# Three quarters of w_out among x's pages and the fourth behind its second reading, the last T copied out of four tiles by two engines, and loads released by the table's landing

## The chip, the cores and the metric

The kernel runs on one core of a Trainium2 chip. The metric is device time in microseconds (us); "before" is the tuned kernel, "after" the same kernel with the change. TensorE is PE (its weight loads PEld), VectorE is DVE, ScalarE is ACT, GpSimd is POOL, and SP is the engine that issues nearly all DMAs.

## The reference

All in float32, with the three parts chained:

```
X = fft(fft(x, axis=1), axis=2).real        # x: [8, 3072, 256] -> 24576 rows of 256
logits = X @ phi                            # 8 experts, 4 slots each: 32 columns
d = softmax(logits, over the rows)          # dispatch, per slot
slot_in = d.T @ X                           # [32, 256]
slot_out[e] = relu(slot_in[e] @ w1[e]) @ w2[e]     # w1[e] 256x1024, w2[e] 1024x256
y = softmax(logits, over the slots) @ slot_out     # [24576, 256]
out = (s * relu(y @ w_in)**2 + b) @ w_out   # w_in 256x2048, w_out 2048x256
```

## The kernel before

The transform is never written out. The program has a prologue of about 206 us and a main loop of about 1177 us (lines L1140, L1170 and L1173, which multiply the 24576 rows with w_in and w_out and are not touched by the change). The prologue runs through these stages:

- **x stage** (0 to about 82 us): 24 pages of x (`xb`, 1 MB each, three per batch of the eight) are multiplied by projected phi and transform tables (`vt`, L419), copied to `vts` (L428), transposed (`vq`, L437), copied to `v` (L441), and multiplied by a transform table into `tps` (L472). ACT or DVE copies `tps` to the table T (`tt`, L484 or L486), eight copies a batch. The last batch has a way of its own (`emit_t(B-1)`, L445 to L470): a tile `tpa` (L450), which ACT copies in eight pieces (L454), and a tile `tpb` (L461), which DVE copies in two (L467). Two matmuls of `keep_busy` on a `warm` tile (L194) stand behind them.
- **lp stage** (about 85 to 98): `lp` (L592) multiplies `tt` with the table `ltab` to the logits, in 16 tiles; DVE takes a maximum of each (L605) and ACT copies it (L606).
- **h stage** (99 to 117) and **r stage** (117 to 179): `hp` (L668) and `htp` (L721), then for each n `dps` (L729), DVE's copy `dh` (L734), and the sum `racc` (L744) over x, which is read a second time in pages `xrt`.
- **e stage** (180 to 206): the sum goes to `rsb` (DVE L886 and ACT L887), through `rtp`, `rt`, `sip` and `si` to the experts: `e_up` (`ehp`, L944, ACT's `hs` L949), `e_turn` (`etp`, L965) and `e_down` (`eop`, L976).

All pages (`xb`, `xrt`, `w1t`, `w2t`, `wi`, `wo`) come from one ring of page buffers, and SP issues their DMAs in program order. Each DMA waits until the eighth before it has landed, and until the last reader of its page is through. `ORDER` is a string of the loads in the x stage: `x` a page of x, `w` a quarter of w_out, `s` a store of `ltab`, `r` a page of `xrt`, `l` a piece of `lt`, `h` a part of `htab`; in `todo` stand those of the r stage.

w_out comes in four quarters of 1 MB (`wo_load(k)`, `raw`). Each has side steps, which `side_step` places between other work: DVE takes the two halves of the words apart (L154, L158, L162, L166, L174; `double_steps`), finds their maxima (L227) and scales (L209, L210), ACT casts a high half (L217, twice), DVE forms a low half (L221, twice), and POOL adds the rows into `bias` (L281, four times). The maxima over all four are then joined (`late_steps`: L258, `mx` L262 and L267, L263, L268) beside `e_up`. `htab_fetch` (L363 to L367) loads the second table `htab_t`; POOL's 1x1 memset (L365) in it is what the load waits for.

Of the kernel before, what the change touches and what calls it, by code (L numbers as in the profile page):

```python
# [32 lines left out]
def tile_fft2__then__softmoe__then__act_relu2(  # L33
# [149 lines left out]
    wo, wi, wok, wik, whl = [], [], [], [], []  # L183
# [13 lines left out]
    def wo_load(k):  # L197
        if k % 2 == 0:
            t, kk = page([P, 8, D], F32, "wo")
            wo.append(t)  # L200
            wok.append(kk)
            whl.append(page([P, 8, 2, D], F16, "whl")[0])
        w = wo[k // 2][:, 4 * (k % 2):4 * (k % 2) + 4, :]
# [29 lines left out]
        steps += [(0.0, lambda j=j: low(j), 0.65) for j in range(2)]  # L233
# [67 lines left out]
    ORDER = "xxxwxxxxxxwxxxxxxwxxxxwxsrllhh"  # L301
    tpool = tc.alloc_tile_pool(name="tpool", bufs=1)
    doubles += [((3, 1, 3, 1)[k], lambda k=k: wo_load(k)) for k in range(4)]
# [88 lines left out]
    with tc.tile_pool(name="xtp", bufs=1, side="right") as xtp, tc.tile_pool(name="vp", bufs=1, side="right") as vp, \  # L392
# [52 lines left out]
        def emit_t(b):  # L445
            bg, bq = divmod(b, NG)
            if b == B - 1:
                t = psv.tile([P, 4, P], F32, tag="vq", name="tpa", bufs=2)
                for k in range(4):
                    nc.tensor.matmul(t[:, k, :], lhsT=vs[bg][:, bq, 4 * k:4 * k + 4, :].rearrange("p j n -> p (j n)"),  # L450
                                     rhs=f_sb, start=True, stop=True)
                for j in range(4):
                    for c in range(2):
                        nc.scalar.copy(tt[64 * bg + NR * c:64 * bg + NR * c + NR, :, bq, 8 * j:8 * j + 4],  # L454
                                       t[NR * j:NR * j + NR, :, 64 * c:64 * c + 64].rearrange("p e k -> p k e"))
                t = psv.tile([P, 2, 4, 64], F32, tag="vt", name="tpb", bufs=2)
                for k in range(4, 8):
                    for j in range(4):
                        for c in range(2):
                            q = 64 * (j // 2) + NR * c  # L460
                            nc.tensor.matmul(t[q:q + NR, j % 2, k - 4, :], lhsT=vs[bg][:, bq, 4 * k + j, :],  # L461
                                             rhs=f_sb[:, 64 * c:64 * c + 64], start=True, stop=True,
                                             tile_position=(0, q), skip_group_check=True)
                for eh in range(2):
                    src = t[64 * eh:64 * eh + 64].rearrange("p j k m -> p m j k")
                    dst = tt[64 * bg:64 * bg + 64, :, bq, 16 * eh:16 * eh + 16].rearrange("p m (j k) -> p m j k", j=2)
                    nc.vector.tensor_copy(dst[:, :, :, 4:8], src)  # L467
# [29 lines left out]
        keep_warm(psv.tile([P, 4 * P], F32, tag="vt", name="warm", bufs=2)[:, :P], 16)  # L497
# [31 lines left out]
        nc.gpsimd.tensor_copy(ltabs[1][0][0:64], ltabs[0][0][64:P])  # L529
# [3 lines left out]
        load_xr()  # L533
        nc.gpsimd.tensor_copy(ltabs[1][0][64:P], ltabs[0][0][0:64])
# [6 lines left out]
        keep_busy(psv.tile([P, 4 * P], F32, tag="vt", name="warm", bufs=2), 4 * P)  # L541
        keep_busy(psv.tile([P, 4 * P], F32, tag="vt", name="warm", bufs=2), P)
# [39 lines left out]
    with tc.tile_pool(name="ps_l", bufs=6, space=PSUM) as psl:  # L582
# [33 lines left out]
        side_step(0.0, True)  # L616
# [18 lines left out]
    with tc.tile_pool(name="ps_h", bufs=3, space=PSUM) as psh:  # L635
# [25 lines left out]
        for i in range(-3, NCH + 1):  # L661
# [170 lines left out]
    todo += [(1, load_xr)] * 2  # L832
# [18 lines left out]
    for n in range(NST + 2):  # L851
# [12 lines left out]
        if n in (1, 2):  # L864
            side_step(0.0, True)
# [463 lines left out]
```

## Time and profile before

| | |
|---|---|
| time of three runs (us) | 1384.62 median, 1384.21 to 1385.57 |
| profiled execution: its own time, its span (us) | 1384.65, 1382.8 |
| busy in the span: PE, DVE, ACT, POOL | 99%, 85%, 73%, 17% |
| mean granted TensorE clock | 0.999 |
| HBM read, written (MB) | 78.50, 26.21 |

The span runs from the first to the last instruction; the profiled execution's own time is 1.85 us longer than it. Busy shares are means over prologue and main loop, and a busy PE need not be PE at its peak. Nearly all the reading from HBM falls in the prologue, so the sections below speak of stretches of the prologue alone.

### The profile page before, as it was taken

To read this page: it belongs to the slowest core of one execution; us is meant where nothing else is said; L and a number is where in the kernel's file an instruction comes from. 1 tells how busy PE (TensorE), PEld (TensorE's weight loads), DVE (VectorE), ACT (ScalarE), POOL (GpSimd) and SP (SyncE) were. 2 spreads that over 40 slices of the span, in tenths; PEclk is the share of its full clock that TensorE was granted. 3 is DMA by queue.
4 is the path that set the end of the run, shared out by engine and by line. 5 is a ranking of instruction groups with operands and counts; after the bars stand their busy time and mean duration, and the time that the engine had idled before them with its cause. 6 is when DMAs were issued, how large, how long until landed. Compare 5 with 4: busy or idle time off the path is not lost.

```text
span 1382.8 us, 22960 instructions
## 1 busy us (share of the span) xinstructions
PE 1366.6 (99%) x8974; PEld 829.6 (60%) x8974; DVE 1171.4 (85%) x1491; ACT 1007.4 (73%) x1413; POOL 231.4 (17%) x287
## 2 busy tenths in 40 slices
PE   8999999999999999999999999999999999999998
PEld 6666555656656666566666666665666666656665
DVE  2587828998989898989898989989888989888886
ACT  2785128877878777877777877777777777777774
POOL 1246001121212121212121211111111111111110
PEclk9999999999999999999999999999999999999999
DMA  9989980101010101010101010110101010101000
GB/s 384 412 312 405 416 349 24 28 24 34 24 36 21 37 24 37 23 35 22 35 24 35 22 37 24 29 29 24 36 21 37 21 36 23 38 24 34 23 22 29
DMA packets 72460, 112.27 MB, mean 81 GB/s; under 512 B 34096, under 2 KB 59696, under 8 KB 64928
## 3 DMA queue, kind: packets, MB, share of 16 engines
q1 hardware_dynamic: 72320, 110.78, 23.0%
q8 instruction: 70, 1.15, 0.3%
q14 instruction: 38, 0.31, 0.1%
q0 software_dynamic: 32, 0.03, 0.0%
HBM read 78.50 MB, written 26.21 MB: 76 GB/s over the span
## 4 chain that ended last, share of the span: by engine, by line
PE 89%; DMA 8%; DVE 2%; SPq 1%; ACT 0%; issue 0%; DVEq 0%; ACTq 0%
PE op L1170 47%; PE op L1173 24%; PE fhp L1140 12%; DMA xb<-in_x_turned_dram 3%; PE racc L744 3%; DMA w2t<-in_moe_w_dram 2%; DMA raw<-in_moe_w_out_dram 1%; PE hp L668 1%; DMA lt<-in_ltab_dram 1%; PE dps L729 1%; DVE cm L605 1%; SPq L1103 0%; DMA ltab<-lt 0%; DVE r L1146 0%; DVE rhl L1131 0%
## 5 line engine op out<-in xcount | busy, mean ns | idle before, releaser
L1170 PE MATMUL op<-whl,rhl 128*128 128x512 f16 x3072 | 1025.5, 379 | 0.8 <-ACT rhl L1130 0.6
L1173 PE MATMUL op<-whl,rhl 128*128 128x256 f16 x3072 | 836.2, 273 | 0.0
L1145 ACT ACTIVATE r<-fhp,wsc 128x768 f32<-128x768 f32 (+1 forms) x513 | 461.4, 900 | 230.8 <-PE fhp L1140 229.8
L1146 DVE SCALAR_TENSOR_TENSOR r<-fhp,r 128x768 f32<-128x768 f32 (+1 forms) x513 | 488.5, 952 | 114.1 <-ACT r L1145 104.0
L1131 DVE TENSOR_TENSOR rhl<-r,rhl 128x768 f16<-128x768 f32 x511 | 506.1, 990 | 0.9 <-ACT rhl L1130 0.9
L1170 PEld LDWEIGHTS <-rhl 128*128 128x128 f16 x3072 | 299.7, 98 | 336.6 <-ACT rhl L1130 0.9
L1130 ACT CAST rhl<-r 128x768 f16<-128x768 f32 x511 | 420.2, 822 | 1.8 <-DVE r L1146 1.8
L1173 PEld LDWEIGHTS <-rhl 128*128 128x128 f16 x3072 | 300.6, 98 | 62.3 <-issue 0.3
L1185 POOL TENSOR_TENSOR ot<-ot,bias 128x256 f32<-128x256 f32 x189 | 137.9, 730 | 974.4 <-DVE ot L1183 974.4
L1140 PE MATMUL fhp<-ct,g 128*128 128x384 f16 x1024 | 250.8, 326 | 1.1 <-DMA g<-gs 0.8
L1140 PEld LDWEIGHTS <-g 128*128 128x128 f16 x1024 | 99.8, 98 | 69.1 <-issue 1.5
L1182 ACT ACTIVATE o<-op,small 128x256 f32<-128x256 f32 x189 | 89.7, 475 | 16.5 <-PE op L1173 16.5
L1183 DVE SCALAR_TENSOR_TENSOR ot<-op,small,o 128x256 f32<-128x256 f32 x192 | 91.4, 476 | 0.3
L419 PE MATMUL vt<-xb,phd 128*64 128x384 f32 (+3 forms) x288 | 47.6, 467 | 4.3 <-DMA xb<-in_x_turned_dram 3.9
L744 PE MATMUL racc<-xrt,dh 128*64 128x256 f32 x384 | 44.5, 383 | 0.4 <-DVE dh L734 0.4
L419 PEld LDWEIGHTS vt<-xb,phd 128*64 128x64 f32 x288 | 25.3, 137 | 24.5 <-issue 7.5
L744 PEld LDWEIGHTS racc<-xrt,dh 128*64 128x64 f32 x384 | 26.3, 137 | 20.9 <-issue 4.1
L486 ACT COPY tt<-tps 32x512 f32<-32x512 f32 x48 | 27.7, 576 | 5.1 <-PE tps L472 4.6
L441 DVE COPY v<-vq 128x512 f32<-128x512 f32 (+1 forms) x15 | 8.3, 593 | 23.8 <-PE vq L437 23.8
L428 ACT COPY vts<-vt 128x512 f32<-128x512 f32 (+1 forms) x15 | 8.0, 535 | 27.6 <-PE vt L419 27.5
L791 POOL TENSOR_TENSOR lg<-lg,rm 112x512 f32<-112x512 f32 x16 | 22.4, 1405 | 5.8 <-DVE rm L789 5.8
L773 POOL TENSOR_TENSOR lg<-et,lg 112x512 f16<-112x512 f32 x16 | 18.5, 1159 | 0.0
(234 smaller groups left out, 480.8 us busy)
## 6 DMA issues: line engine op xcount, KB each, us to landing
xb<-in_x_turned_dram SPq DMA_DIRECT2D x24, 1024.0 KB, 20.2
xrt<-in_x_pages_dram SPq DMA_DIRECT2D x24, 1024.0 KB, 11.6
out_dram<-ot SPq DMA_DIRECT2D x128, 128.0 KB, 1.7
w1t<-in_moe_w_dram SPq DMA_DIRECT2D x8, 1024.0 KB, 13.8
out_dram<-ot SPq DMA_DIRECT2D x128, 64.0 KB, 2.0
raw<-in_moe_w_out_dram SPq DMA_DIRECT2D x4, 1024.0 KB, 20.3
raw<-in_moe_w_in_dram SPq DMA_DIRECT2D x4, 1024.0 KB, 9.3
w2t<-in_moe_w_dram SPq DMA_DIRECT2D x4, 1024.0 KB, 16.8
```

Of the source, the lines that this page charges most:

```text
L419: nc.tensor.matmul(vt[64 * h:64 * h + 64, o:o + k, :], lhsT=phd[:, c, sg, :], rhs=turned(pg, c, i, k, rev), start=(c == 0 and m < 2), stop ...
L744: nc.tensor.matmul(raccs[acc][64 * h:64 * h + 64, :], lhsT=dh[:, m, g].rearrange("p j e -> p (j e)"), rhs=xr[k][0][:, g, t, :], start=(sum ...
L1130: nc.scalar.copy(a, r2)
L1131: nc.vector.tensor_tensor(out=l, in0=r2, in1=a, op=ALU.subtract)
L1140: nc.tensor.matmul(hp[k * split][:, k, :].rearrange("p (s b m) -> p s b m", s=2, b=B), lhsT=g16[:, f * P:(f + 1) * P], rhs=c, start=True, ...
L1145: nc.scalar.activation(out=r[:, k], in_=hp[i][:, k], func=AF.Relu, scale=wsc[:, 2, p:p + 1])
L1146: nc.vector.scalar_tensor_tensor(out=r2[:, k], in0=hp[i][:, k], scalar=0.0, in1=r[:, k], op0=ALU.max, op1=ALU.mult)
L1170: nc.tensor.matmul(op.rearrange("p h d -> p (h d)"), lhsT=a, rhs=w.rearrange("p h d -> p (h d)"), start=(f == 0), stop=False)
L1173: nc.tensor.matmul(op[:, 0, :], lhsT=l, rhs=w[:, 0, :], start=False, stop=(f == NFC - 1))
L1182: nc.scalar.activation(out=o1, in_=op[:, 1, :], func=AF.Copy, scale=qv)
L1183: nc.vector.scalar_tensor_tensor(out=ot, in0=op[:, 0, :], scalar=qv, in1=o1, op0=ALU.mult, op1=ALU.add)
L1185: nc.gpsimd.tensor_tensor(out=ot, in0=ot, in1=bias, op=ALU.add)
```

## The change

Five edits, all in the prologue.

1. `ORDER` has three `w` in place of four, the first behind the eighth `x` of the string instead of the third. Quarter 4 (k = 3) is loaded in `todo`, behind the last `xrt` and ahead of the first `w1t`. Quarters 3 and 4 have `wo` pages of their own; the low halves of quarter 3 go to steps 8 and 10 of the h stage.
2. `emit_t(B-1)` uses two tiles `tpa` and two tiles `tpb`; ACT and DVE each copy one of either kind.
3. In `htab_fetch` the 1x1 memset is a 1x1 copy from `ltabs[0]`, and POOL's first copy of `ltab` comes behind the loads instead of ahead of them.
4. The warm-up at the start is 28 matmuls with 64 moving columns instead of 16 with 128; the two `keep_busy` ahead of `lp` are gone.
5. The side step behind `mt` and those at n = 1 and 2 of the r stage are gone, and the `late_steps` stand further back in the e stage.

```diff
-        w = wo[k // 2][:, 4 * (k % 2):4 * (k % 2) + 4, :]
+        w = wo[0][:, 4 * k:4 * k + 4, :] if k < 2 else wo[k - 1]
...
-        steps += [(0.0, lambda j=j: low(j), 0.65) for j in range(2)]
+        if k == 2:
+            late_low.extend(lambda j=j: low(j) for j in range(2))
+        else:
+            steps += [(0.0, lambda j=j: low(j), 0.65) for j in range(2)]
...
-    ORDER = "xxxwxxxxxxwxxxxxxwxxxxwxsrllhh"
+    ORDER = "xxxxxxxxwxxxxxxwxxxwxxxsrllhh"
...
-        nc.gpsimd.memset(t[0:1, 0, 0, 0:1], 0.0)
+        nc.gpsimd.tensor_copy(t[0:1, 0, 0, 0:1], ltabs[0][0][0:1, 0, 0:1])
...
-                t = psv.tile([P, 4, P], F32, tag="vq", name="tpa", bufs=2)
+                for m in range(2):
+                    t = psv.tile([P, 4, P], F32, tag="vq", name="tpa", bufs=2)
...
+                    for j in range(4):
+                        for c in range(2):
+                            r = 64 * bg + NR * c
+                            (nc.vector.tensor_copy if m else nc.scalar.copy)(
+                                tt[r:r + NR, :, bq, 8 * j + 2 * m:8 * j + 2 * m + 2],
+                                t[NR * j:NR * j + NR, 0:2, 64 * c:64 * c + 64].rearrange("p e k -> p k e"))
+                ts = [psv.tile([P, 2, 4, 64], F32, tag="vt", name="tpb", bufs=2) for _ in range(2)]
...
-                    nc.vector.tensor_copy(dst[:, :, :, 4:8], src)
+                    (nc.vector.tensor_copy if eh else nc.scalar.copy)(dst[:, :, :, 4:8], src)
...
-        keep_warm(psv.tile([P, 4 * P], F32, tag="vt", name="warm", bufs=2)[:, :P], 16)
+        keep_warm(psv.tile([P, 4 * P], F32, tag="vt", name="warm", bufs=2)[:, :P // 2], 28)
...
-        nc.gpsimd.tensor_copy(ltabs[1][0][0:64], ltabs[0][0][64:P])
         for i in range(2):
             htab_fetch(i)
         load_xr()
         load_xr()
+        nc.gpsimd.tensor_copy(ltabs[1][0][0:64], ltabs[0][0][64:P])
...
-        keep_busy(psv.tile([P, 4 * P], F32, tag="vt", name="warm", bufs=2), 4 * P)
-        keep_busy(psv.tile([P, 4 * P], F32, tag="vt", name="warm", bufs=2), P)
...
+            if i in (8, 10):
+                late_low.pop(0)()
...
-    todo += [(1, load_xr)] * 2
+    todo += [(1, load_xr)] * 2 + [(2, lambda: wo_load(3))]
...
-        if n in (1, 2):
-            side_step(0.0, True)
...
-    late_steps.pop(0)()
     for eg in range(2):
         for fh in range(2):
             e_up(eg, fh)
-            late_steps.pop(0)()
             e_side(2.0)
...
+            if eg + fh:
+                late_steps.pop(0)()
```

Three engines' orders show what this moves. **DVE** at the end of the r stage, before (`dh` is the last copy of the r stage, `rsb` the first of the e stage; line numbers differ by up to ten between the kernels):

```order
L245 TENSOR_REDUCE small<-wi 128x1
L258 TENSOR_REDUCE small<-small 128x1
L734 COPY dh<-dps 128x2x4x32
L879 TENSOR_SCALAR small<-zacc 128x1
L880 RECIPROCAL small<-small 128x1
L263 TENSOR_REDUCE small<-mx 1x1
L886 TENSOR_SCALAR rsb<-racc_1156,small 128x256
```

And in the changed kernel:

```order
L740 COPY dh<-dps 128x2x4x32
L154 TENSOR_SCALAR wo<-raw 128x1024
L158 SCALAR_TENSOR_TENSOR wo<-raw,wo 128x1024
L162 SCALAR_TENSOR_TENSOR wo<-raw,wo 128x1024
L883 TENSOR_SCALAR small<-zacc 128x1
L884 RECIPROCAL small<-small 128x1
L166 TENSOR_SCALAR raw<-raw 128x1024
L174 SCALAR_TENSOR_TENSOR wo<-raw,wo 128x1024
L228 TENSOR_REDUCE wsc<-wo 128x2
L890 TENSOR_SCALAR rsb<-racc_1158,small 128x256
```

Six steps of quarter 4 now stand between the last `dh` and `rsb`. Behind `si` DVE's changed order goes on with the rest of that quarter and the joined maximum:

```order
L917 COPY si<-sip 128x64
L210 TENSOR_SCALAR wsc<-wsc 128x2
L211 RECIPROCAL wsc<-wsc 128x2
L222 SCALAR_TENSOR_TENSOR whl<-wo,wsc,whl 128x2x256 x2
L262 TENSOR_REDUCE small<-wsc 128x1
L262 TENSOR_REDUCE small<-small 128x1
L267 TENSOR_REDUCE small<-mx 1x1 x2
```

Before, L258 stood directly behind `si`. **POOL** around the table, before:

```order
L281 TENSOR_TENSOR bias<-bias,wo 128x256 x4
L529 COPY ltab<-ltab 64x2048
L365 MEMSET htab_t 1x1 x2
L534 COPY ltab<-ltab 64x2048
L281 TENSOR_TENSOR bias<-bias,wo 128x256 x4
```

And in the changed kernel, there and then in the e stage, where the last four bias additions now stand behind `sel`:

```order
L285 TENSOR_TENSOR bias<-bias,wo 128x256 x4
L369 COPY htab_t<-ltab 1x1 x2
L540 COPY ltab<-ltab 64x2048
L541 COPY ltab<-ltab 64x2048
L375 COPY htab_t<-htab_t 48x16x52
```

```order
L797 TENSOR_TENSOR lg<-lg,rm 112x512
L932 DMA sel_sb<-in_sel_dram 128x2x32
L934 COPY sel_1775<-sel_sb 128x256
L285 TENSOR_TENSOR bias<-bias,wo 128x256 x4
L1112 COPY g_2000<-gs 32x320 x4
```

The 1x1 copies stand ahead of both copies of `ltab`, and the additions have moved past the h and r stages. **SP** at the second weights `w2t`, with what each DMA waits for (DMAHW0 to DMAHW7 are the landings of the eighth DMA before), before:

```order
L826 DMA w2t<-in_moe_w_dram 128x2048 [waits DMAHW7_49,PE_49]
L826 DMA w2t<-in_moe_w_dram 128x1024 [waits DMAHW0_49,PE_49]
L826 DMA w2t<-in_moe_w_dram 128x1024 [waits DMAHW1_49,PE_49]
L826 DMA w2t<-in_moe_w_dram 128x1024 [waits DMAHW2_49,PE_49]
L826 DMA w2t<-in_moe_w_dram 128x1024 [waits DMAHW3_49,PE_49]
L826 DMA w2t<-in_moe_w_dram 128x1024 [waits DMAHW4_49]
```

And in the changed kernel:

```order
L832 DMA w2t<-in_moe_w_dram 128x2048 [waits DMAHW7_49,PE_49]
L832 DMA w2t<-in_moe_w_dram 128x1024 [waits DMAHW0_49,DVE_49]
L832 DMA w2t<-in_moe_w_dram 128x1024 [waits DMAHW1_49,DVE_49,Pool_49]
L832 DMA w2t<-in_moe_w_dram 128x1024 [waits DMAHW2_49,PE_49]
L832 DMA w2t<-in_moe_w_dram 128x1024 [waits DMAHW3_49]
L832 DMA w2t<-in_moe_w_dram 128x1024 [waits DMAHW4_49]
```

The second of the half-size `w2t` loads takes the page of quarter 4 in `wo`: it waits for that quarter's low halves on DVE and its bias additions on POOL.

## Rows read from the trace of the kernel before

**Rows 1.** Busy time by stretch: us, then each engine's busy (count), clock, DMA share, GB/s.
```profile
6.00:78.00 72.00, 67.69 (x459) 44.72 (x459) 36.71 (x55) 40.94 (x72) 12.53 (x15) 1.00 1.02 414
96.00:200.00 104.00, 101.93 (x893) 62.60 (x895) 67.38 (x113) 36.41 (x67) 25.51 (x24) 1.00 1.01 408
```
**Rows 2.** The chain that ended last: start us, us, what.
```profile
79.00 4.71 DMA ltab<-lt
...
193.85 9.60 DMA w2t<-in_moe_w_dram
203.48 1.93 PE eop L976 x26
```
**Rows 3.** PE alone in two stretches of the start: us, PE busy, clock, DMA share, GB/s.
```profile
0.75:5.84 5.09, 4.83 (x22) 1.00 0.79 258
5.84:7.15 1.31, 1.29 (x12) 1.00 0.99 386
```
**Rows 4.** Timeline of the x stage: start us, us, engine, line, operation; [idle before <- releaser].
```profile
7.15 1.11 PE L492 MATMUL pp<-phi_sb,dd 128*128 128x64 f32 x8
...
28.26 2.04 PE L419 MATMUL vt<-xb,phd 128*64 128x384 f32 x9 [2.89 <-DMA xb<-in_x_turned_dram]
...
71.30 3.65 PE L419 MATMUL vt<-xb,phd 128*64 128x512 f32 x16
```
**Rows 5.** PE's waits in the x stage: line, what was waited for, us in total, times, longest.
```profile
PE vt L419 <- DMA xb<-in_x_turned_dram: 3.9, 3, 2.9
```
**Rows 6.** Timeline from the last T to the loads behind the table.
```profile
76.97 4.69 ACT L484 COPY tt<-tps 32x512 f32<-32x512 f32 x8 [0.41 <-PE tps L472]
...
82.23 2.98 ACT L454 COPY tt<-tpa 32x256 f32<-32x256 f32 x8 [0.57 <-PE tpa L450]
...
83.18 1.67 PE L194 MATMUL warm<-dd,ones 128*128 128x512 f32 x4
...
84.10 1.90 POOL L529 COPY ltab<-ltab 64x2048 f32<-64x2048 f32 x1 [12.83 <-DMA ltab<-lt]
...
85.26 4.30 PE L592 MATMUL lp<-tt,ltab 64*64 64x128 f32 x130 [0.41 <-ACT tt L454]
...
86.08 1.65 SPq L366 DMA_DIRECT2D htab_t<-in_htab_dram  x2
```
**Rows 7.** Timeline: the steps of one quarter of w_out, in the x and lp stages.
```profile
62.90 0.68 DVE L154 TENSOR_SCALAR wo<-raw 128x1024 uint32<-128x1024 uint32 x1
...
64.88 1.23 DVE L162 SCALAR_TENSOR_TENSOR wo<-raw,wo 128x1024 uint32<-128x1024 uint32 x1
...
69.91 1.33 ACT L217 ACTIVATE whl<-wo,wsc 128x512 f16<-128x512 f32 x2 [0.70 <-DVE wsc L210]
...
72.09 1.41 DVE L221 SCALAR_TENSOR_TENSOR whl<-wo,wsc,whl 128x512 f16<-128x512 f32 x2
...
88.12 3.14 POOL L281 TENSOR_TENSOR bias<-bias,wo 128x256 f32<-128x256 f32 x4
```
**Rows 8.** Timeline of the r stage's end.
```profile
173.80 0.42 DVE L734 COPY dh<-dps 128x256 f32<-128x256 f32 x1 [0.23 <-PE dps L729]
...
179.54 0.48 DVE L886 TENSOR_SCALAR rsb<-racc,small 128x256 f32<-128x256 f32 x1 [1.65 <-PE racc L744]
```
**Rows 9.** Timeline of the e stage.
```profile
183.42 1.92 PE L944 MATMUL ehp<-w1t,si 128*32 128x512 f32 x16
...
185.46 1.09 ACT L949 ACTIVATE hs<-ehp 128x512 f32<-128x512 f32 x1 [2.76 <-PE ehp L944]
...
189.42 0.39 POOL L930 COPY sel<-sel_sb 128x256 f32<-128x256 f32 x1 [4.94 <-DMA sel_sb<-in_sel_dram]
...
202.81 0.14 PEld L976 LDWEIGHTS eop<-w2t,hT 128*32 128x32 f32 x2 [1.05 <-DMA w2t<-in_moe_w_dram]
```
**Rows 10.** SP's queue there, and PE alone in the e stage's second part.
```profile
179.51 8.70 SPq L826 DMA_DIRECT2D w2t<-in_moe_w_dram  x3
...
190.00:206.00 16.00, 15.02 (x170) 1.00 0.80 315
```

More of the change, by code (lines that the diff above doesn't have):

```diff
@@ L181, in double_steps @@
         return [(0.0, s1, 0.65), (0.0, s2, 1.15), (0.0, s3, 1.15), (0.0, s4, 0.65), (0.0, s5, 0.0 if pool else 1.15)]
-    wo, wi, wok, wik, whl = [], [], [], [], []
+    wo, wi, wok, wik, whl, late_low = [], [], [], [], [], []
     wa, wra, wim = [small[:, k:k + 1] for k in range(3)]
@@ L197, in wo_load @@
     def wo_load(k):
-        if k % 2 == 0:
-            t, kk = page([P, 8, D], F32, "wo")
+        if k != 1:
+            t, kk = page([P, 4 if k else 8, D], F32, "wo")
             wo.append(t)
             wok.append(kk)
+        if k % 2 == 0:
             whl.append(page([P, 8, 2, D], F16, "whl")[0])
-        w = wo[k // 2][:, 4 * (k % 2):4 * (k % 2) + 4, :]
+        w = wo[0][:, 4 * k:4 * k + 4, :] if k < 2 else wo[k - 1]
         hl = whl[k // 2][:, 4 * (k % 2):4 * (k % 2) + 4]
@@ L222, in low @@
                                            in1=hl[:, 2 * j:2 * j + 2, 0, :], op0=ALU.mult, op1=ALU.subtract)
-            if j and k % 2:
-                drop(wok[k // 2])
+            if j and k:
+                drop(wok[k - 1])
         steps = double_steps(d, w_out.rearrange("(k p) d -> p k d", p=P)[:, 4 * k:4 * k + 4, :], False)
@@ L300, in tile_fft2__then__softmoe__then__act_relu2 @@
     LEAD, TOL, LT, LX, HX = 14.0, 0.5, 0, 0, 1
-    ORDER = "xxxwxxxxxxwxxxxxxwxxxxwxsrllhh"
+    ORDER = "xxxxxxxxwxxxxxxwxxxwxxxsrllhh"
     tpool = tc.alloc_tile_pool(name="tpool", bufs=1)
-    doubles += [((3, 1, 3, 1)[k], lambda k=k: wo_load(k)) for k in range(4)]
+    doubles += [((3, 1, 3)[k], lambda k=k: wo_load(k)) for k in range(3)]
     order = list(ORDER)
@@ L447, in emit_t @@
             if b == B - 1:
-                t = psv.tile([P, 4, P], F32, tag="vq", name="tpa", bufs=2)
-                for k in range(4):
[L450 to L457, printed above, removed]
+                for m in range(2):
+                    t = psv.tile([P, 4, P], F32, tag="vq", name="tpa", bufs=2)
+                    for k in range(2):
+                        nc.tensor.matmul(t[:, k, :], rhs=f_sb, start=True, stop=True,
+                                         lhsT=vs[bg][:, bq, 8 * m + 4 * k:8 * m + 4 * k + 4, :].rearrange("p j n -> p (j n)"))
+                    for j in range(4):
[5 more added lines that the diff above has]
+                ts = [psv.tile([P, 2, 4, 64], F32, tag="vt", name="tpb", bufs=2) for _ in range(2)]
+                for k in range(4):
                     for j in range(4):
@@ L460, in emit_t @@
                             q = 64 * (j // 2) + NR * c
-                            nc.tensor.matmul(t[q:q + NR, j % 2, k - 4, :], lhsT=vs[bg][:, bq, 4 * k + j, :],
+                            nc.tensor.matmul(ts[j // 2][q:q + NR, j % 2, k, :], lhsT=vs[bg][:, bq, 16 + 4 * k + j, :],
                                              rhs=f_sb[:, 64 * c:64 * c + 64], start=True, stop=True,
@@ L1009, in tile_fft2__then__softmoe__then__act_relu2 @@
                     pass
+            if eg + fh:
+                late_steps.pop(0)()
+            if (eg, fh) == (0, 1):
                 while len(wim_steps) > 1:
@@ L1033, in tile_fft2__then__softmoe__then__act_relu2 @@
     e_down(0, 0)
+    late_steps.pop(0)()
     e_turn(1, 0)
     e_down(0, 1)
+    late_steps.pop(0)()
     e_turn(1, 1)
```

3 lines of the change are left out of this document (1 added, 2 removed).

## The prediction

> **What bounds the kernel now.** I read the shares by stretch first, then the chain of work that ended last, then the timelines at the three places where the chain changes hands. By the shares, the DMA engines are saturated in the x stage (DMA share 1.02, 414 GB/s) while PE is busy 67.69 of 72 us; in the h, r and e stages both are full: PE 101.93 of 104 us, DMA 1.01 [rows 1]. Behind that the main loop is PE's. So only the prologue can give or lose time, and whatever its end moves by, the whole program moves by. The chain shows what ends it: the table's landing (79.00 + 4.71 = 83.71) in the x stage, and at the end the `w2t` pages, whose last large one lands at 203.48, with 26 matmuls of `eop` behind it (1.93, to 205.41) [rows 2]. DMA is thus the bound at the end by a little, with PE close behind: PE is idle 0.98 of the 16 us from 190 to 206 [rows 10], while its weight loads show a single wait for `w2t` of 1.05 [rows 9]. I put PE's slack there at 1.0 to 2.0 us.
>
> **The change part by part.** Sums are against the profiled execution, 1384.65 us, that is its span of 1382.8 and 1.85 around it; it stands 0.03 above the median of the runs.
>
> *The stream of loads.* A quarter of w_out is 1.05 MB, at 414 GB/s [rows 1] 2.5 us. Three instead of four ahead of the last page of x: that page, `lt` and `ltab` land 2.5 earlier, `ltab` at 81.2. Today `htab` is issued at 86.08, after POOL's copy of `ltab` (84.10 to 86.00) [rows 6]; with the 1x1 copies ahead it is issued as soon as POOL sees the landing, 84.10 - 2.5 and some 0.1, so about 81.7: 4.4 earlier. Everything behind it in SP's queue gains 4.4 until the fourth quarter is put back ahead of `w1t` (2.5): from there the stream leads by 1.9.
>
> *The start.* The old warm-up's 32 passes (a float32 matmul runs as two) end at 7.15, when `pp` starts [rows 4]. Up to 5.84 there are 22 passes in 4.83 us, 0.22 each; behind it 12 in 1.29, 0.11 each [rows 3]: the pace doubles, 1.2 to 2.4 GHz, though the clock column prints 1.00 for both. The new passes move half as many columns but load the same 128 columns of weights. `pp` has that very shape, 128x64, and takes 1.11 for 8, 0.14 each [rows 4], not less than the 128x128 passes at the upper level. So I take the pace as unchanged: 22 of 56 passes by 5.84, 34 more by 0.11, end at 9.6, x stage 2.5 later. The other bound is that a pass takes half as long throughout: end near 5.5 to 7, no delay. I take the first, being the nearest row. The delay is covered: PE waits 3.9 us for x in that stage [rows 5], and the pages now come earlier. The last batch, which starts at 71.30 [rows 4], would start at 71.30 + 2.5 - 3.9 = 69.9.
>
> The Trainium skill's page "TensorE: Matmul & The Clock Gate", section "LDWEIGHTS (loading the stationary operand)", says that a weight load takes a time that goes with its columns alone, about the columns over 1.2 in ns. By it 128 columns cost 107 ns a pass, which the 0.11 of the upper level agrees with and the 0.22 of the lower does not; held to throughout, 56 passes would end at 7.0.
>
> *The last T.* ACT must first cast the third quarter, whose steps now fall here. From DVE's L162 to ACT's cast are 64.88 to 69.91, 5.03, and the cast takes 1.33 [rows 7]. L162 can start 0.9 to 1.8 behind the last batch's start (two 512-wide `v` copies lie ahead, 0.6 each if they take as long as L484's, 4.69 / 8, and PE's transposes end a little either side of that start): cast at 75.8 to 76.8, done 77.1 to 78.1; the eight `tt` copies of the seventh batch 4.69; the new `tpa` copies are half of 2.98 / 8 = 0.37 wide [rows 6], about 0.27 each by the difference between the 256 and 512 wide ones, so 2.1; one `tpb` copy, 512 wide, 0.6. T is whole at 84.5 to 85.5; today `lp` starts at 85.26 [rows 6]. What the two engines save is taken by the cast: gain of 0.7 to a loss of 0.2, taken as 0. `ltab`, at 81.2, is long there.
>
> *The two `keep_busy`.* They run in 83.18 to 84.85 while PE would wait [rows 6], so taking them away saves nothing directly. But PE then stands still from the end of `tpb`, about 81.8, to `lp`: some 3.4 us (in the old kernel 0.41 [rows 6]). The longest such gap that this trace shows with the clock unharmed is 2.89 [rows 4]. Rival A.
>
> *The low halves in the h stage, the side steps taken out.* Two of 0.7 (1.41 / 2) [rows 7] on DVE, whose share in 96 to 200 is 67.38 of 104 [rows 1] while PE is the bound: 0, at most 0.2 if one falls ahead of an evacuation.
>
> *The end of the r stage.* DVE has six steps of the fourth quarter between the last `dh` (ends 174.22) and `rsb` (179.54) [rows 8]: L154 0.68, L158 and L162 1.23 each [rows 7], L166 0.69, L174 and L227 1.22 each by their shapes, 6.3, and the two small ones 0.34, with gaps 6.8 in all. `rsb` comes at 181.0: +1.46. PE waits for it, because everything to the experts hangs on it.
>
> *The e stage.* Now `mx` needs the fourth quarter's maximum, which DVE's order has behind its two low halves. Those need ACT's casts, which stand behind the first `hs`. Counted from `ehp`'s start (183.42 before, so 184.88): `hs` starts 2.04 later and takes 1.09 [rows 9], the cast 1.33, the last low half 0.7, two reductions 0.35: 5.5 behind `ehp`'s start, while `ehp`'s 32 passes keep PE for 2 x 1.92 less some overlap, 3.6 to 3.8. PE stands still for about 1.9, with `e_up(1,0)` and all of `e_turn` behind it. With 0.2 for the new order of the small matmuls, PE's own account is 1.46 + 1.9 + 0.2 = 3.56, less the slack of 1.0 to 2.0: +1.6 to +2.6.
>
> *SP's queue.* The second half-size `w2t` load now waits for POOL. Today it is one of three issued between 179.51 and 188.21 [rows 10]. POOL's additions stand behind `sel` (189.42, 0.39) [rows 9], which moves with the stage by 1.46, and take 3.14 [rows 7]: end at 194.4, issue at 194.5. Behind it up to the last 256 KB piece are 3.41 MB, 8.2 us at 414 GB/s, and the fixed part of a landing, 4.71 for `ltab`'s 1 MB less its 2.5, 2.2 [rows 2]: landed at 204.9, against 203.48. Add 1.93: 206.85, +1.45. So the lead of 1.9 is lost in the wait, and more. The bounds: if `sel`, which waits 4.94 for its DMA behind other traffic [rows 9], lands 2.5 sooner in an emptier queue, this account falls to -1.0, and PE's alone decides.
>
> **Sum:** the larger of both accounts, PE's lower end or the queue's, +1.6 and +1.45: 1384.65 + 1.6 = **1386.2 us**. 0.2% of the time, about what a measurement of this kernel can tell from no change, is 2.8 us; so no measurable change.
>
> **The rivals.**
>
> *A, the clock falls (slower).* In the uncovered gap before `lp` TensorE drops to 1.2 GHz. For it: the gap is longer than any that the trace shows survived. Against: it is longer by only 0.5. Price: at the start the upper level came 4.83 us after the first pass [rows 3]. `lp` has 256 passes over 16 tiles, 0.55 us of PE a tile at the upper level (130 passes in 4.30 [rows 6]), about DVE's pace; at the lower 1.1. In 4.8 us 4.4 tiles instead of 8.7, about 2.3 us lost, nothing hides them: 1384.65 + 1.6 + 2.3 = 1388.5. It decides if the fall comes at a gap of under about 3.4. The Trainium skill's same page, section "HAM oscillation — how this bites in real kernels", tells of kernels whose TensorE falls to the lower level while waiting for data between short bursts; nothing in this trace shows a fall.
>
> *B, the fourth quarter hides.* Its steps fit into DVE's idle time and the queue's lead of 1.9 reaches the last `w2t`. For it: DVE is idle a third of the r stage. Against: the order has the steps between `dh` and `rsb`, where they can't slip forward. 1384.65 - 1.9 = 1382.7.
>
> *C, the warm-up is no longer than before.* If the new passes take half, the x stage starts on time. The last T could then be whole up to 2.5 earlier, but the pages of x hold PE again as today (3.9 us of waits [rows 5]); I take 1.0 of the 2.5. The r and e stages start as much earlier, and PE's account falls to +0.6: 1385.2. For it: half as many columns move. Against: `pp`'s 0.14 in the same shape.
>
> **How the numbers follow.** Forecast 0.52, A 0.20, B 0.10, C 0.18. The range reaches from B to A with PE's upper end in it: 1382.7 to 1389.0. Slower by over 0.2% is A and the tail of the forecast (+2.6 and a little): 0.25. Faster by over 0.2% needs more than B gives: 0.07. Within: 0.68. By the Trainium skill's weight-load rule alone the sum would be C's.
>
> **What would show it.** Warm-up's end near 9.6 (C: 7). `htab` issued near 81.7. `lp` at about 85.3, its passes at the upper level (A: 1.1 a tile). `rsb` about 1.5 later relative to the last `dh`. A gap of about 1.9 on PE ahead of `mx` in the e stage. The second half-size `w2t` issued near 194.5, the last `eop` ended near 206.9. The forecast is wrong if `lp` starts more than 1.5 off, or if the last `w2t` lands well before 204 and PE does not stand still at `mx`.

## Result, and the profile after

| | before | after |
|---|---|---|
| time, median (us) | 1385.09 (4 runs, 1384.21 to 1386.07) | 1398.94 (4 runs, 1397.19 to 1399.26) |
| span of the profiled execution (us) | 1382.8 | 1397.2 |
| ratio, 95% interval | | 1.0098 [1.0083, 1.0113] |

The change made the kernel 13.9 us slower; 1386.2 was forecast, in a range up to 1389.0. Reading the first start of the same work in both timelines shows where the span's 14.4 us lie:

| up to the start of | before | after | late by | added there |
|---|---|---|---|---|
| end of `tpb` (x stage) | 83.24 | 87.76 | 4.52 | 4.52 |
| `lp` | 85.26 | 91.41 | 6.15 | 1.63 |
| `hp` | 99.62 | 106.71 | 7.09 | 0.94 |
| `htp` | 114.45 | 122.41 | 7.96 | 0.87 |
| `rtp` | 180.07 | 189.13 | 9.06 | 1.10 |
| `e_up(1,0)` | 187.63 | 200.93 | 13.30 | 4.24 |
| `gp` (start of the main loop's work) | 206.90 | 220.24 | 13.34 | 0.04 |
| end of the span | 1382.8 | 1397.2 | 14.4 | 1.06 |

The last 1.06 falls at the start of the main loop, where PE waits 1.9 us for the landings of `g` instead of 0.8.

The timeline of the changed kernel at these places (start us, us, engine, line, operation; idle before and its releaser):

```profile
1.01 12.21 PE L190 MATMUL warm<-ones 128*128 128x64 f32 x56 [1.01 <-POOL ones L339]
...
75.74 3.65 PE L423 MATMUL vt<-xb,phd 128*64 128x512 f32 x16
...
80.76 3.15 POOL L285 TENSOR_TENSOR bias<-bias,wo 128x256 f32<-128x256 f32 x4 [2.33 <-DVE wo L174]
...
82.56 1.33 ACT L218 ACTIVATE whl<-wo,wsc 128x512 f16<-128x512 f32 x2 [2.18 <-DVE wsc L211]
...
83.92 4.68 ACT L491 COPY tt<-tps 32x512 f32<-32x512 f32 x8
84.06 0.81 SPq L370 DMA_DIRECT2D htab_t<-in_htab_dram  x2
...
86.64 1.12 PE L468 MATMUL tpb<-f_sb,v 128*32 128x64 f32 x64
...
91.41 10.00 PE L597 MATMUL lp<-tt,ltab 64*64 64x128 f32 x256 [3.65 <-ACT tt L474]
...
115.22 4.23 POOL L649 TENSOR_TENSOR dt<-lg,cmb 112x512 f32<-112x512 f32 x2 [0.51 <-PE hp L672]
115.31 0.75 DVE L222 SCALAR_TENSOR_TENSOR whl<-wo,wsc,whl 128x512 f16<-128x512 f32 x1
...
188.60 0.47 DVE L890 TENSOR_SCALAR rsb<-racc,small 128x256 f32<-128x256 f32 x1
189.13 1.10 PE L908 MATMUL rtp<-stack,rsb 128*128 128x64 f32 x8 [1.68 <-DVE rsb L890]
...
193.56 5.86 PE L948 MATMUL ehp<-w1t,si 128*32 128x512 f32 x32
...
199.87 3.58 POOL L285 TENSOR_TENSOR bias<-bias,wo 128x256 f32<-128x256 f32 x4
...
200.73 0.27 PE L266 MATMUL mx<-ident,small 128*1 128x128 f32 x1 [1.32 <-DVE small L262]
```

PE alone in stretches of the changed kernel (us, PE busy, granted clock, DMA share, GB/s):

```profile
5.84:13.00 7.16, 7.16 (x35) 1.00 1.01 414
92.50:94.00 1.50, 1.50 (x36) 0.50 1.05 431
94.00:96.00 2.00, 2.00 (x52) 0.58 0.98 361
191.00:193.00 2.00, 2.00 (x11) 0.56 1.07 436
193.00:195.00 2.00, 2.00 (x11) 0.50 1.01 416
```

And the end of its chain (start us, us, what):

```profile
203.47 0.33 SPq L832
...
206.74 10.04 DMA w2t<-in_moe_w_dram
216.82 1.93 PE eop L980 x26
```

The reader is to see: the warm-up's passes take 0.218 from the first to the last; where [rows 3] changed pace at 5.84, these 35 keep the lower one (the column prints 1.00 in both). `lp` starts after 3.65 of standstill, against 0.41 in [rows 6], and the granted clock behind it is 0.50, the lower level. It falls again at 191, behind 1.68 of waiting for `rsb`, and the 32 `ehp` passes take 5.86, where in [rows 9] 16 took 1.92. The last T is late on ACT: the cast of the third quarter stands ahead of `tt`. SP's wait on POOL is there as foreseen: the additions end at 203.45, the `w2t` load goes at 203.47, and the chain that ended last runs through it.

### The profile page after: what moved, and what is told of

It reads as the page before. It is cut to its first block, busy times and chain, and to the rows that moved or that the text cites. A ratio compares the mean times of both kernels' runs of the same rounds, so it can differ in the third digit from the quotient of the medians.

```text
span 1397.2 us, 22999 instructions
## 1 busy us (share of the span) xinstructions
PE 1377.0 (99%) x8994; PEld 842.0 (60%) x8994; DVE 1181.4 (85%) x1510; ACT 999.0 (71%) x1402; POOL 233.8 (17%) x287
## 4 chain that ended last, share of the span: by engine, by line
PE 82%; DMA 1%; DVE 1%; SPq 1%; ACT 0%; issue 0%; ACTq 0%; DVEq 0%
PE op L1177 47%; PE op L1180 24%; PE fhp L1147 12%; DMA w2t<-in_moe_w_dram 1%; SPq L1110 1%; DVE r L1153 0%; DVE rhl L1138 0%; SPq L832 0%; PE eop L980 0%; PE gp L1081 0%; ACT r L1152 0%; DMA g<-gs 0%; PE gr L1094 0%; DVE ot L1190 0%; DVE g L1087 0%
## 5 line engine op out<-in xcount | busy, mean ns | idle before, releaser
L423 PE MATMUL vt<-xb,phd 128*64 128x512 f32 (+3 forms) x288 | 49.3, 485 | 0.4 <-DVE phd L501 0.4
L423 PEld LDWEIGHTS vt<-xb,phd 128*64 128x64 f32 x288 | 28.3, 142 | 18.6 <-issue 11.9
L493 ACT COPY tt<-tps 32x512 f32<-32x512 f32 x32 | 18.4, 576 | 6.1 <-PE tps L479 5.7
```

Of the source, the lines that this page charges most:

```text
L423: nc.tensor.matmul(vt[64 * h:64 * h + 64, o:o + k, :], lhsT=phd[:, c, sg, :], rhs=turned(pg, c, i, k, rev), start=(c == 0 and m < 2), stop ...
```

## Experiments

All times are medians, in us; the kernel before was timed beside each group and gave 1385.0 to 1385.3.

| run | time | ratio to before, interval |
|---|---|---|
| e1: changed, old warm-up | 1390.16 | 1.0042 [1.0027, 1.0056] |
| e2: changed, 28 warm-ups of 128 columns | 1394.39 | 1.0075 [1.0050, 1.0100] |
| e3: changed, keep_busy back | 1402.14 | 1.0126 [1.0109, 1.0143] |
| e4: changed, two matmuls in the wait for rsb | 1397.56 | 1.0092 [1.0077, 1.0107] |
| e5: e1 and keep_busy on a free tile | 1391.43 | 1.0051 [1.0038, 1.0063] |
| e6: e5 and low halves in the r stage | 1391.55 | 1.0043 [1.0029, 1.0056] |
| e7: before, last T and early loads | 1388.70 | 1.0027 [1.0017, 1.0037] |
| e8: before, new warm-up | 1394.06 | 1.0066 [1.0052, 1.0080] |
| e9: before, last T | 1387.80 | 1.0018 [1.0009, 1.0027] |
| e10: before, early loads | 1387.41 | 1.0015 [1.0006, 1.0025] |
| e11: e6, loads let go by the first lp tile | 1389.11 | 1.0028 [1.0018, 1.0039] |
| e12: before, moves of the quarters | 1392.35 | 1.0047 [1.0034, 1.0059] |
| e13: e11, bias additions sooner | 1388.38 | 1.0026 [1.0016, 1.0037] |
| e14: before, htab early, x pages held | 1385.29 | 1.0002 [0.9993, 1.0011] |
| e15: e13, a fourth side step | 1388.30 | 1.0024 [1.0015, 1.0033] |

### The start: e1, e2, e8

```diff
-        keep_warm(psv.tile([P, 4 * P], F32, tag="vt", name="warm", bufs=2)[:, :P // 2], 28)
+        keep_warm(psv.tile([P, 4 * P], F32, tag="vt", name="warm", bufs=2)[:, :P], 16)    # e1; 28 in e2; the reverse, on the kernel before, in e8
```

> The changed kernel with the old warm-up (16 matmuls of 128 moving columns). Theory T1: the new warm-up's 64-column passes never raise TensorE's clock, and this makes the x stage late; in the changed kernel the passes took 0.218 us from first to last (12.21 for 56) and the last batch started at 75.74 instead of 71.30. With the old ones the pace doubles near 5.8 again, warm-up ends near 7.1, tpb ends 4 to 5 us earlier than its 87.76, and the time falls by 4 to 5 us to about 1394. Rival R1 (my prediction's step): the x stage absorbs a late start in its waits for pages, so the start is worth under 1.5 us and the 14 us come from behind it: 1397.5 to 1399. The clock would still fall ahead of lp under both.

> The changed kernel with 28 warm-up matmuls, but of 128 moving columns. It tells the number of passes from their width. T1 (it is the width): the pace doubles near 5.8 as in the kernel before, 34 passes at 0.107 end the warm-up at 9.5, the x stage starts 2.5 later than with 16 and about 5 to 6 earlier than in the changed kernel; time within 1.5 us of the run with 16, about 1394 to 1395.5. Rival: so many passes ahead of the x stage cost by their number, the clock stays low for some other reason, and the time is that of the changed kernel, 1398 to 1399.

> The kernel before with the new warm-up alone (28 matmuls of 64 columns). Theory T1: the passes take 0.218 to the end (12.2), the x stage starts at 15.3 instead of 8.64 at the lower level, its 3.9 us of waits for pages are used up, the last batch starts 3 to 4.5 us late, and the time rises by 3 to 5 to 1388 to 1390 (more if the fall of the clock at lp comes with it). Rival R1: the waits take it all, under 1.5 more.

e1 gave 8.8 us back, more than the 4 to 5 of T1: `tpb` came 5.6 earlier (81.01), and the second fall of the clock, in the e stage, was not there. e8 added 8.7 to the kernel before. Not all of that is the start: `lp` begins 4.57 later there (89.83) and then stands still twice, 3.2 us together, with nothing waited for; the section on the standstill inside `lp` takes this up. The timeline of e8's start and that of e2:

```profile
1.01 12.21 PE L190 MATMUL warm<-ones 128*128 128x64 f32 x56 [1.01 <-POOL ones L335]
13.01 1.92 PE L492 MATMUL pp<-phi_sb,dd 128*128 128x64 f32 x8
```

```profile
1.01 9.38 PE L190 MATMUL warm<-ones 128*128 128x128 f32 x56 [1.01 <-POOL ones L339]
10.22 1.00 PE L499 MATMUL pp<-phi_sb,dd 128*128 128x64 f32 x8
```

The same number of passes ends 2.83 sooner when they are twice as wide, so the start at the lower level came with the narrower passes, not with their number. In e2 `tpb` stands at 81.17, 0.16 behind e1: a start that is 3 us late only because of its passes is swallowed by the waits for x, as the prediction had it. A start at the lower level isn't: in the changed kernel `pp` (1.91 instead of 1.11) and most of the first batch of the x stage ran at it too, and only behind them the pace was that of the kernel before. The first batch, before and after:

```profile
8.64 5.81 PE L419 MATMUL vt<-xb,phd 128*64 128x512 f32 x36 [0.38 <-DVE phd L494]
```

```profile
15.31 8.40 PE L423 MATMUL vt<-xb,phd 128*64 128x512 f32 x36 [0.38 <-DVE phd L501]
```

The x stage starts 6.67 late and is 9.26 late behind its first batch. PE's waits for x, 3.9 before [rows 5], are all gone, and 4.52 is left at `tpb`.

The other half of e2's expectation failed: its median is 4.2 above e1, with single times of 1391.67, 1393.07, 1395.70 and 1399.96. The mean granted clock of these four falls in the same order, 0.999, 0.997, 0.996, 0.995, which points to more time at the lower level in the longer ones. Where that was stays open, since the profiled execution is the fastest of them.

### The standstills: e3, e4, e5

```diff
+        keep_busy(psv.tile([P, 4 * P], F32, tag="vt", name="warm", bufs=2), 4 * P)      # e3, two of them, as before
...
+        for _ in range(2):                                                              # e5
+            keep_busy(psv.tile([P, 8, P], F32, tag="tps", name="warm", bufs=2).rearrange("p a b -> p (a b)"), 4 * P)
...
+    keep_busy(w0, 4 * P)                                                                # e4, ahead of rtp
+    keep_busy(w0, 2 * P)
```

> The changed kernel with the two keep_busy matmuls ahead of lp put back. Theory T2: TensorE's standstill of 3.65 us between tpb and lp lowers the clock (granted 0.50 from 92.5 to 94); with the two back the clock stays at the upper level through lp, the lp stage takes 14.4 from lp's first to hp's first instead of 15.3, and the time falls by about 0.9 to 1398.0. Rival: the two only fill 1.7 of the 3.7 us, the clock falls anyhow, no change (1398.9); or the fall has its cause in the slow start and stays.

> The changed kernel with two more matmuls of ones (512 and 256 columns, results unused) on TensorE while it waits 1.68 us for rsb at the end of the r stage. Theory T3: the second fall of the clock (granted 0.50 to 0.56 from 191 to 197) comes from that standstill and costs about 3 us: sip 1.70 instead of 1.08, the first 32 ehp passes 5.86 instead of 4.0. Filled, the clock stays up there, e_up(1,0) starts 2.5 to 3 us earlier after rtp, and the time falls by 2 to 3 to about 1396.4. Rival: the time in the e stage is set by the fourth quarter's chain (cast, low halves, maxima, POOL's additions, w2t) and not by TensorE's pace; then ehp gets faster but mx waits longer, and the time falls by under 1.

> The changed kernel with the old warm-up, and with two 512-column keep_busy matmuls between tpb and lp on a free tps tile (their old vt tile is taken by the new second tpb, so that they had waited for its copies and held lp up by 1.8). With the old warm-up alone lp starts at 84.35 and hp at 100.55: 16.2 for the lp stage, against 14.36 before, with the clock at 0.56 to 0.59 from 84 to 88. Theory T2: filled, the clock stays up, the lp stage takes 14.4, and the time falls by 1.8 from 1390.2 to 1388.4. Rival: lp's stage is DVE's (cm 0.6 a tile), the clock fall cost little and the lp stage stays near 16: 1390.

e3 lost 3.2 us instead of gaining 0.9. Its timeline:

```profile
90.97 2.17 PE L194 MATMUL warm<-dd,ones 128*128 128x512 f32 x4 [3.66 <-ACT tt L474]
...
93.20 5.01 PE L599 MATMUL lp<-tt,ltab 64*64 64x128 f32 x127
```

Both `vt` tiles now hold `tpb`, so the filling matmuls wait for the very copies whose wait they were to fill, and then stand ahead of `lp`, which starts 1.79 later than in the changed kernel (91.41). The rest of the loss comes behind that: `lp` stands still twice with no releaser ("issue"). PE's waits in e3, and the same in e8 (us, times, longest):

```profile
PE lp L599 <- issue: 3.2, 2, 1.7
```

```profile
PE lp L592 <- issue: 3.2, 2, 2.0
```

e4 agrees with T3 in its profile; its median is 1.4 below the changed kernel's, with intervals that overlap:

```profile
186.87 1.56 PE L194 MATMUL w<-dd,ones 128*128 128x512 f32 x4
188.61 1.10 PE L911 MATMUL rtp<-stack,rsb 128*128 128x64 f32 x8 [0.19 <-DVE rsb L890]
...
191.90 3.64 PE L951 MATMUL ehp<-w1t,si 128*32 128x512 f32 x32
```

e5's filling worked up to 89 us, and yet nothing was gained: TensorE then stood still for 1.82 us in the middle of `lp`, as in e3 and e8 released by nothing that the profile shows. That was the open question, and T2 alone didn't answer it.

### The standstill inside lp: e6, e7, e9, e10, e11, e12, e14

> As the run before, and quarter 3's two low halves moved from the h stage (steps 8 and 10) to the r stage (n = 3 and 4). Theory T4: in the changed kernel POOL's two subtractions in the h stage took 4.23 us instead of 2.55 while DVE's low halves ran beside them, PE's hp waited for dt, and the h stage took 15.70 instead of 14.83; moved, it takes 14.83 and the time falls by 0.9. Rival: the h stage is longer for another reason, or the r stage gives the 0.9 back, since its POOL work stands beside the low halves there: within 0.3 of the run before.

> The kernel before with the last T in four tiles by two engines and the loads let go by the table's landing, and nothing else of the change (keep_busy, two of 512 columns, on a free tps tile). Theory T5: these two edits are not what costs; lp starts 0 to 1 us earlier than 85.26, htab is issued 1.8 or more earlier than 86.08, and the time is 1384 to 1385.5, no change. Rival: the 32x128 copies (2.41 us for eight on DVE, 2.13 on ACT, against 2.98 for eight of double width) and the second tpb copy on ACT cost more than they spare, lp starts 1 us later, 1386.

> The kernel before with the last T in four tiles alone (keep_busy on a free tps tile; the loads behind the table as before). With this and the earlier loads together, lp began at 87.01 instead of 85.26, DVE's copies ending last, and then TensorE stood still for 2.99 us in lp with nothing waited for, while a 16 KB packet of the instruction queue, at 86.32 in the kernel before, came only at 92.95. Theory T6: the standstill is the fetch of TensorE's instructions, which waits in the DMA engines behind the x pages that the earlier loads put there; the T edit alone costs its 1.7 at lp's start and no standstill: about 1387. Rival: the standstill comes with the T edit (more instructions on TensorE, another place of the boundary): 1388.5 and the packet again beyond 90.

> The kernel before with the loads let go by the table's landing alone. T6: htab and the x pages start about 1.8 us earlier, the instruction packet that came at 86.32 comes behind them at 89 or later, TensorE stands still in lp for 1.5 to 3 us, the clock falls behind it, and the time rises by 2 to 4 to 1387 to 1389. Rival (my prediction's step): earlier loads are a lead or nothing: 1384 to 1385.5, the packet at 86 to 87.

> The changed kernel with the old warm-up, keep_busy ahead of lp, the low halves in the r stage (1391.5 so far), and the loads of htab and the x pages behind it let go by the first lp tile's copy instead of by the table. T6: the instruction packet that came at 90.05 comes at 85 to 87 again, lp runs through, hp starts about 3 us earlier than its 102.31, the time falls by 2.5 to 3.5 to about 1388.5. Rival: the standstill does not hang on these loads, hp stays at 102 or is later because htab is: 1391 or more.

> The moves of w_out's quarters and what goes with them alone (order of loads, fourth quarter behind the last x page, low halves in the h stage, later maxima); warm-up, last T, keep_busy and the table's loads as in the kernel before. From the traces: h stage +0.9, rsb +1.1 net, e stage from ehp to gp +2.3, start of the main loop 0 to 1; together +4.3 to +5, 1389.5 to 1390.5, if lp starts at 84 to 85.5 and has no standstill. T6 says no standstill as long as the queue is empty when the instruction packet is asked for, but with the table 2.5 earlier the loads start 2.5 earlier too (83.6), which may be too early: then 1392 to 1393. Rival (my prediction): +1.6, 1386.6.

> The kernel before with htab let go by the table's landing (as in the change), and only the x pages behind it held until ScalarE has copied the first lp tile, so that the instruction packet finds an empty queue. T6: the packet comes at 85.5 to 87, no standstill in lp, hp starts at 99.6 as before, the stream of pages from there on is 0.5 to 1.5 us earlier, and as the last w2t sets the end with 1 us of PE slack, the time is 1384 to 1385: not told from before, or 0.05 to 0.1% better; against 1387.4 with the pages let go as well. Rival: htab's own 0.6 MB is enough to hold the packet up: 1386.5 to 1387.5.

e6 and e11 move these lines (e9, e10 and e12 are the hunks of the change's diff):

```diff
+        if n in (3, 4):                        # e6, in the r stage instead of the h stage
+            late_low.pop(0)()
...
+            if st == 0:                        # e11, in lp's loop instead of ahead of the last T
+                for i in range(2):
+                    htab_fetch(i)              # its 1x1 copy now reads lg, which ACT has copied from the first lp tile
+                load_xr()
+                load_xr()
```

The page of the kernel before has the clue, in the instruction counts and in the DMA queues (packets, MB, share):

```profile
PE 1366.6 (99%) x8974; PEld 829.6 (60%) x8974; DVE 1171.4 (85%) x1491; ACT 1007.4 (73%) x1413; POOL 231.4 (17%) x287
...
q8 instruction: 70, 1.15, 0.3%
```

70 packets of 16 KB for 17948 instructions of TensorE (matmuls and weight loads) are one packet for 256 of them, that is 128 passes with their weight loads. The 256 passes of `lp` take 9 us, so by this count they use up a packet in 4 to 5 (an estimate; part of it can have been fetched ahead, as the packets before come at 79.0, 86.3 and 94.3). Queues of the stretch 82 to 89, in the kernel before, in e6, and in e11:

```profile
q1 hardware_dynamic: 135, 0.79, 41.5%
q8 instruction: 1, 0.02, 0.9%
```

```profile
q1 hardware_dynamic: 154, 0.84, 68.0%
```

```profile
q1 hardware_dynamic: 22, 0.15, 10.5%
q8 instruction: 1, 0.02, 0.9%
```

Before, the packet comes at 86.3, between the table and `htab`, when the engines have nothing to move. In e6 the loads start earlier, fill the engines, and the packet is not among the 154; it comes at 90.05. The timeline of e6, and its clock:

```profile
89.16 0.84 PE L599 MATMUL lp<-tt,ltab 64*64 64x128 f32 x19 [0.18 <-ACT lg L613]
...
92.46 4.92 PE L599 MATMUL lp<-tt,ltab 64*48 64x128 f32 x107 [2.47 <-issue]
```

```profile
90.00:92.00 2.00, 0.00 (x0) 1.00 1.01 410
92.00:94.00 2.00, 1.54 (x52) 0.93 0.98 393
94.00:96.00 2.00, 2.00 (x44) 0.50 0.98 381
```

e11 changes when the loads are let go, and the packet is back (at 86.06), `lp` runs through, and the clock stays up:

```profile
84.44 4.27 PE L591 MATMUL lp<-tt,ltab 64*64 64x128 f32 x130 [0.47 <-DVE tt L474]
88.90 4.58 PE L591 MATMUL lp<-tt,ltab 64*64 64x128 f32 x126 [0.18 <-ACT lg L605]
```

Its time is 2.4 below e6's, `hp` starts at 98.77 instead of 102.31. In the runs where `lp` stands still, it goes on 1.2 to 1.5 us after the packet's transfer has ended (e6: 90.05 and 1.11 for the transfer, on at 92.46; e7: 92.95 and 1.08, on at 95.33). T6 holds from the other side too. e7, with the last T and the early loads on the kernel before, refutes its T5: `lp` starts 1.75 later, stands still for 2.99, and the time rises by 3.4. Early loads alone (e10) on the kernel before: no packet in 82 to 89, 1.93 of standstill, +2.1 us. The quarters alone (e12), which let the loads go earlier as well, in its waits (us, times, longest):

```profile
PE lp L596 <- issue: 2.9, 1, 2.9
```

The last T alone (e9) starts `lp` at 86.91, which is 1.65 later because DVE, behind the fourth quarter's steps, now has copies of `tpa` (2.41) ahead of its `tpb`; the packet comes behind the first loads here too, at 90.96: 1.54 of standstill, +2.5 us. There the expectation was wrong in saying that no standstill would come with it. In e14 the packet came at 88.57, not at 85.5 to 87: `htab` alone holds it up by some 2 us, `lp` stood still for 0.79, and the gain in the stream (a `w2t` end 0.9 later than before, not earlier) was none: 1385.29, not told from before. In e8 the loads go as before (`htab` at 85.87), but `lp` starts late: the packet comes at 94.02, and `lp` stands still as well. That fits T6, by which it counts whether the packet is called for ahead of the loads or behind them; the trace shows when it moves, not when it is called for.

e6's own question is answered by its trace: the h stage, from `hp` to `htp`, takes 14.83 as before, against 15.70 with DVE's low halves in it. The time didn't show it, since the standstill in `lp` grew from 1.82 to 2.47 and the second fall of the clock was back (0.50 from 186 to 192).

### What was left: e13, e15

```diff
+        steps.append((0.0, lambda: bias_add(k, d.rearrange("p (k d) -> p k d", d=D)), 0.0))     # e13, ahead of the maxima
...
         if n >= 6:                                                                             # e15, in the r stage
             side_step(0.0, True)
             side_step(0.0, True)
+            side_step(0.0, True)
```

> The run with the late loads (1389.1; start, lp and h stage mended), and the fourth quarter's bias additions ahead of its maxima, so that POOL makes them before sel instead of behind it. It takes away the wait that my prediction took for the end of the prologue: the second half-size w2t is issued near 189 to 190 instead of 193.0 (behind sel's 189.49 and 3.14 of additions). Theory T7: in that run the w2t pages land back to back (199 to 209.2) in a stream that is 3.7 us later at the first w1t than before (169.4 against 165.8), since a quarter lies ahead of them and the loads begin at 87.2; so the wait on POOL binds nothing and the time stays at 1389 within 0.7. Rival (my prediction): it binds, the last w2t lands 3 earlier, 1386 to 1387.

> As the run before, and four side steps instead of three per step of the r stage, so that all of the fourth quarter's DVE work up to its low halves lies ahead of rsb and six of its steps ahead of the last dh. PE's two standstills of 1.68 (rtp for rsb) and 1.69 (mx) go. T7: the w2t stream sets the end, so PE only waits longer for w2t (2.6 us so far) and the time falls by under 1: 1388.3 to 1389. Rival T8: the e stage's cost is PE's standstills; the time falls by 2.5 to 3.4 to 1385.7 to 1386.6.

The wait on POOL goes in e13 (the second half-size `w2t` is issued at 187.6 instead of 193.0), and 0.7 us with it; PE's wait for `rsb` is down to 0.43 there already. In e15 it is 0.17, the standstill at `mx` is gone, and the time falls by 0.1 us. The intervals tell neither 0.7 nor 0.1 from nothing. In these runs the prologue's end is the stream's. e15's waits of PE from 176 to 213, and then the stretches 81 to 90 of e15 and of the kernel before (us, PE busy, clock, DMA share, GB/s):

```profile
PE eop L984 <- DMA w2t<-in_moe_w_dram: 2.8, 3, 1.9
PE mx L271 <- DVE small L267: 0.4, 1, 0.4
```

```profile
81.00:90.00 9.00, 8.21 (x231) 1.00 0.24 48
90.00:200.00 110.00, 103.91 (x944) 1.00 1.01 403
```

```profile
81.00:90.00 9.00, 8.18 (x215) 1.00 0.56 157
90.00:200.00 110.00, 107.75 (x1022) 1.00 1.01 404
```

From 90 on the engines are full in both. From 81 to 90 they are busy 0.24 of the time instead of 0.56: (0.56 - 0.24) x 9 = 2.9 us of transfers are missing, and the first `gp` starts 3.05 later (209.95 against 206.90). In these runs the quarter taken out ahead of the table only let the DMA engines stand idle longer, because the loads behind it are held until `lp` has fetched its instructions, and then the quarter has to be carried behind.

## Why the prediction failed

- **The start: the step that failed.** "So I take the pace as unchanged: 22 of 56 passes by 5.84, 34 more by 0.11, end at 9.6." The pace at the lower level was unchanged, the rise didn't come: end at 13.2, and `pp` and most of the first batch of the x stage went on at the lower level. The term was an x stage 2.5 late, covered by PE's waits; it measured 6.67, and 9.26 behind the first batch, of which 4.52 was left uncovered at `tpb`. e1 gives 8.8 us for the warm-up as a whole. That more passes alone are covered held (e2: 0.16 at `tpb`). Rival C, the shorter warm-up, was furthest from the trace. The Trainium skill's page "TensorE: Matmul & The Clock Gate", section "LDWEIGHTS (loading the stationary operand)", gives the time of a weight load as its columns over 1.2 in ns, 107 for 128 columns by that (an estimate), with no mention of the clock. The passes at the upper level agree (0.11 [rows 3]); at the lower level the trace disagrees: there passes with 128 stationary columns took 218 ns, whether 64 or 128 columns moved.
- **The missing term.** No step of the prediction asked how TensorE gets its instructions. The part of the change that looked free, loads 4.4 earlier and a lead of 1.9, is what makes it wait in `lp`: 1.5 to 3.0 us in e5, e6, e7, e10 and e12, and behind that the clock fell in each of these. A later `lp` does the same (1.5 in e9 and 3.2 in e8, both with the loads as before; 3.2 in e3). In the changed kernel itself it didn't show: the packet (93.5) was in time. Why it was, when in e3, with `lp` 1.8 later, it came at 97.5 and too late, stays open. The Trainium skill's page "Runtime: NRT & Kernel Launch", section "Instruction fetch mechanics", says that blocks of 256 instructions are fetched through a DMA queue of the engine's own and that this is mostly hidden. The 256 agrees with the counts of the profile; hidden it was, in these runs, only where the loads left the packet room.
- **Rival A** happened, behind the standstill ahead of `lp`: the lower level from about 92.3 to 95.7, 0.94 us in the lp stage instead of the priced 2.3. The price took `lp`'s pace as halved for 4.8 us; it fell by a fifth, 36 passes in 1.50 against 130 in 4.30 [rows 6], and for a shorter time. It also happened where nothing was foreseen, in the e stage (`sip` 1.70 instead of 1.08, two `e_up` 5.86 instead of 4.0).
- **The last T** was taken as 0 and cost 1.63: ACT's cast, put at 75.8 to 76.8, began at 82.56, since the batches came late and DVE's steps of the third quarter with them (L162 at 77.54; the 5.03 from there to the cast held). With the start mended (e1) `lp` begins at 84.35, 0.15 before the earliest end that the prediction gave for T, 84.5.
- **The loads.** `htab` went at 84.06, not 81.7: POOL had bias additions ahead of the 1x1 copies until 83.9. In e1 it went at 81.12.
- **`rsb` and `mx`** were right as mechanisms. `rsb` started 6.41 behind the end of the last `dh` instead of 5.32, 1.09 later where 1.46 was foreseen, and PE waited 1.68 for it instead of 0.23. At `mx` PE stood still for 1.32 (1.9 foreseen), partly by luck: at the lower level the reductions ended 7.0 behind the start of `ehp` (5.5 foreseen) and the 32 passes took 5.86 (3.6 to 3.8 foreseen). At the upper level the wait was 1.69 (e11). e15 shows that they do not set the time once the rest is mended.
- **SP's wait on POOL** was there, its load issued 0.02 behind the last addition, at 203.47 where 194.5 was foreseen, since the e stage came late. What it costs in the changed kernel itself was not run. With the start, `lp` and the h stage mended it is worth 0.7 (e13), not told from nothing; what ends the prologue there is the stream, which has lost its lead at the table.
- **The low halves in the h stage**, taken as 0 to 0.2, cost 0.87: POOL's subtractions beside them took 4.23 for two.

The parts don't add: the warm-up (e8, +8.7), the quarters (e12, +7.0), the last T (e9, +2.5) and the early loads (e10, +2.1) come to 20.3 alone, 13.9 together. Each of the four has a standstill in `lp`, 9.6 us in all, that the changed kernel doesn't have; how the rest overlaps was not taken apart. No version here beats the kernel before; e14 equals it.

## What to carry to other kernels

Before a warm-up is replaced by more and smaller passes, look in the trace at whether the pace of its own passes still doubles. Before transfers are started earlier, look at what else uses the DMA engines in the gap they had left; an idle stretch may be the time in which the busiest engine gets its instructions, and "issue" waits in a dense run of small matmuls with no releaser are its sign. And where a matmul fills a wait, look up whose buffer it writes: after tiles are split, the filling may wait for what it was to bridge.

## What was not expected of the hardware

- 56 passes over 64 columns in 12.2 us without a pause left TensorE at its lower level; of the same number over 128 columns only the first 22 ran there (9.4 us in all).
- The length of a standstill alone doesn't tell whether the clock falls. In e1 the level fell behind 2.22 us of waiting; the kernel before kept it across 2.89 [rows 4]. The 1.68 ahead of `rtp` came with a fall in the changed kernel and in e6, and without one in e1, e5, e11 and e12; what decides it stays open. PE busy and clock of e1:

```profile
82.00:84.00 2.00, 0.13 (x10) 1.00 1.15 226
84.00:86.00 2.00, 1.65 (x32) 0.59 1.04 146
```

- A 16 KB instruction packet came about 4 us later when `htab` and pages of 1 MB were issued ahead of it (90.05 in e6 against 86.06 in e11), and TensorE went on 1.3 us after the end of its transfer.
- POOL's 112x512 subtraction took about 2.1 us instead of 1.27 with DVE's float16 low halves beside it.
